# Feature sums of the key exponentials: from a DVE reduction to accumulating matmuls with the identity, under a new issue order

## The chip, the cores and the metric

The kernel runs on one core of one Trainium2 chip, as one launch. The metric is the device time of one execution in microseconds. Names of engines: PE is TensorE (PEld is its weight load), DVE is VectorE, ACT is ScalarE, POOL is GpSimd, and SP is the sync engine, which here issues nearly all DMAs.

## The reference

One input `u` (1 x 2048 x 512, bf16) feeds two branches, which a per-position gate mixes:

```python
x = A_u
g = sigmoid((x * gate_w).sum(-1, keepdims=True))
a = A(x, A_re, A_im, B_re, B_im, C_re, C_im, log_dt, Dskip)
b = B(x, wqkv, w_phi, wo)
return g * a + (1 - g) * b

def A(u, ...):                       # D=512, N=128, L=2048
    dt = exp(log_dt)[:, None]
    logdA, dB = dt * (A_re + 1j * A_im), dt * (B_re + 1j * B_im)
    K = einsum("dn,dnl,dn->dl", C, exp(logdA[:, :, None] * l), dB).real
    y = irfft(rfft(u padded to 2L) * rfft(K padded to 2L))[:L]
    return y + u * Dskip

def B(x, ...):                       # 32 heads, Dh=16
    q, k, v = x @ wqkv, split into heads
    pq, pk = q @ w_phi, k @ w_phi                       # per head
    phi_q = concat([softmax(pq), softmax(-pq)])         # over the head's 16 features
    phi_k = concat([softmax(pk), softmax(-pk)])
    kv, z = sum over s of phi_k x v, and of phi_k
    o = (phi_q @ kv) / (phi_q . z + 1e-6)
    return o @ wo
```

The change concerns the softmax denominators of `phi_k`: for each position, head and sign, the sum of 16 exponentials.

## The kernel before, in words

**How the order is made.** Each piece of work is a node of a `Plan` (`P.add(engine, cost, function, dependencies, take=rings, drop=rings)`). The costs and due times serve a planner that has been run beforehand. Its answer stands in the source as three strings: `ORDER` (two base-64 digits a node, the order of issue), `SIDES` (whether ACT or DVE does each eviction of PSUM by `evict`, lines 556 and 558), and `RINGS` (which PSUM ring a node takes: `ps` with two buffers, `p0` with two, `bk` with three, `pf` with two). On the chip each engine works through its own queue strictly in the order that `ORDER` gives; SP's queue of DMA issues is one of them. So a new string moves everything, on all engines.

**The stages**, as the order of before runs them:

- *Setup* (`prepare`, and the first part of `keys_and_spectrum`). SP loads `u` in four pieces (`UD`), loads the parameters B, C, A transposed (`nB`, `nC`, `nA`, line 292), loads the small tables and `Wv`, loads the query and key weights transposed (`wTq`, `wTk`, line 297), and loads `u` transposed as four `xT` blocks. PE multiplies `UD` with a table (`psA`, line 577), the result is evicted to `XAu`, multiplied again (`psB`, line 225), evicted to `XU` and written to a DRAM buffer `XUd`. DVE makes the tables, the parameter products (`pt`, line 425) and the folded key weights `Wkp` (evicted at line 556).
- *Keys* (the loop `for s2 in range(8)`, two tiles of 128 positions each, `u` = 0, 1). `pk` projects a tile (line 695, four matmuls of N=512 into a `bk` bank). `ex` makes two exponentials, exp(pk) and exp(-pk), each 128x512, into `Ek` (128 x 2 tiles x 2 signs x 512). `rd` reduces each 16 features of a head to one number on DVE (line 707), into `Zk`, 128 x 2 x 2 x 32 in fp32. `ln` takes the logarithm of the pair's `Zk` and then exp(-log), i.e. the reciprocal, into the last row of `vr`. `pv` projects the values (`vp`, line 727), an eviction copies them to `vb`, `sc` multiplies `vb` by the reciprocals into `vr` (line 736), and `kn` accumulates `kvp` with 32 small matmuls a tile (line 744).
- *The convolution kernel*, interleaved with the keys and queries: exponentials `E` and cosines `cs` of `args` on ACT, products `R` (lines 998 and 1001) and `A` (line 991) on DVE, and many small matmuls `kps` (line 212), evicted to `KD`.
- *Queries and convolution* (`queries_and_convolution`): query exponentials `Eq`, their denominators (`zs`, line 894), the transforms of the convolution (`psA`, `psB`, `psz` with evictions `XA`, `XK`, `Zr`), DMA round trips through DRAM (`XUd` to `U`, `Zr` to `Zd` to `ZT`), the attention output `bps` (lines 955 and 958), and the gated mix written out (`out_dram`).

The lines that the change touches, and those that call them:

Of the kernel before, what the change touches and what calls it, by code (L numbers as in the profile page):

```python
# [91 lines left out]
class Plan:  # L92


    DIGITS = "0123456789abcdefghijklmnopqrstuvwxyzABCDEFGHIJKLMNOPQRSTUVWXYZ-_"
    ORDER = ("050K0L0O0e0k0b08060v0M0N0001020h0n070f0c0g03090d0a0l0i0o0w0P0T0Q0m0R0y0z0q0B0U0V0S0-0Z0_100W1112132D16172F2H0X0Y141504"
             "18191a1b1c2E2G2I2J2K2L1p0j2M1q1u1t1d1i1e1f2N2P2R1j1r1v1z1s1k0p1w1y1A1B1N2O1E1C2S2Q1D1R1O1F1G1H1S2T1M2U2V2W2X2Z2_2Y1L2-"
             "1K1V1Q1g1T3031321h1l1W1I1U1x1P1m1J1X1Y0A1Z1-0s0x3335373438393a1_203b3c3d3f3e3g21220r3h3i3j3k2327243l3m3n3p3o3q2825292b"
             "2x2d3r3R0t0E0F3s2a2f3t2c2g2h3S2e3u3v3x3y3w2i2j2o2k2p1n2l2q263z3B363C3A2s2m2r0C2t2n0u0H0G2u3D3G3E3F0D2v3P0I0J2y2z3Q453H"
             "3I462A3J3K3M3N3O1o3L3U2B2w3X413V3Y3-442C3T4b4c4e4f4q4r4d4g4i4h4m4t4j4n4u638R8S4k4o4l4x4p4B4s4v474y4C4F424w4I8T4G4J8U97"  # L100
             "3W433Z4z4D4M4Q4R8V4H4K4L4A4E4U8W4N4V4X984O4Y4P4S4T575a585b9c4W4Z595c8X8Y4_494-50515d4a8Z919253545e5f8-93558_945i905j95"
             "963_525g99569a9b9e5m5n9B5k9d5p5q5t5h9f5u5x5l9g5B5o9m9C5r9o9n5s5v9h5y5z5C5D9i9p9r9D5E9E5w5I5M9t9j9k9F5J9l5A5F9q5G9G5Q5T"
             "5N5R9u9s5H5K5O5S5U9H5V9I9v9w5X5_5Y5W9J5Z605L615P9N5-629x9O9y649z9A9K6566aRaS9P6768696b6a406c6d6e6f9T9L9M6g6V9QaW9R9W9U"
             "a29VaPaQaU9S9Xa36h6i6Wa5aTa66j6k486m9Y9ZaX6laVadae6n9-9_a0a4a7aob2b4aYaZap6o6pagaf6qaqa-aha_a8bh6r6X6Za9aaai6s6t6u6vbi"
             "bjbkb0b36w6-b56_706x6Bb1b9arab6ya1b66Casb7b8babl6z6Ybm716Abb72ac73746F6G6D6E6J75atcvcwbc6K6L6H76776Ibdbe6McBajakcxcCbf"
             "bgauavbnbCbobDcDbz6Nbp6O78awbA797abBbEal7ebt7b7c7damanbKbucy7i6P7f6Q7g7j7h7mczbqbV6Rbrbv6T6S6U7k7nbLbMbWaxaybs7o7lbw7y"
             "bxbNbOby7zcE7p7AbF7CcAcMcF7E7B7D7FbPbGbHbI7q7G7Hc4c5bYbZ7IbXb-7J7KcN7L7s7M7NdjcG7Odk7PcP7u7rcHd17tcQ7w7vd2c7bQ7xc8bR7Q"
             "cO8b7RbJ7T7UcV8cbSc67Vc9cI8d8f8hcJ8ecKcRcS8gcT8i8j8kcL7ScUducW8l7W8mcX7XcY8ndl8ob_c0efegcZc_7_dv7Y7Zc-bTbUcad080cbdmdn"
             "8pc1dx7-d3dydw818qelccc2cd8r828s8w8tc3dod4dzeh8u83dp84ce8xdF8v8ydqdr8AdAd5dB8zdsdQ858Ed6d78B8C86dI8FdJ8GdGemen8D878HdR"
             "d8dTdHdKdCdDdEewd9dUexeydSdVdtddeH89deeiej88eIeJ8ada8Idf8KeodL8M8JdM8L8NdNdOdW8OdXdY8P8QazdZekdbepdgeqeresdceuetevf1dh"  # L110
             "aAf4f5cfaCaDezf2f3eAcgfaaBaEaFeKaKeLf6eBeMf7ciaGfbf8f9d-fifocjdPcheCfjeDaLeNckd_e0e2aHaIeOeEePaMclcmfkdifcfdfefgfhfffl"
             "frfmaNfscnaJaOeFeGcofpfncqcrcse1e5fqeQfteReSeVe3cpeTe4eWctfueUeaeXe6ebfwe7e8ecedeefvfxe9cueYeZfyfze-fAe_f0fBfC")
    SIDES = ("0100000011110011000000011000000100000000101110000000100000101000010000010000000100000000010000010000000000000011000000"
             "00000101001")
    RINGS = ("1100101101100100010000000000000000000022222222222222222222222222222222000002222222222222222222222222222222200000000000"
             "0000000000000000000300000000000000000000000300000000000000000000000330030333303330033")

    def __init__(self, rings, psum):
        self.k, self.dyn, self.nodes = dict(rings, **psum), set(psum), []
# [140 lines left out]
def prepare(P, tc, nc, g, evict, psum):  # L260

    fc, act, persist = g.fc, g.act, g.persist
# [20 lines left out]
    P.dma(1.1, 3.0, lambda: g.load_ld(), rw=("", "ldc ldb"))  # L283
    P.add("W", 7.0, lambda: None, rw=("raw0", "raw"))
    for dj in range(4):
        P.dma(0.6, 3.0, lambda dj=dj: g.load_ud(dj), rw=("", f"ud{dj}"), move=2.6)


    def turn(ks):
# [3 lines left out]
    for ks in (("Bre", "Bim"), ("Cre", "Cim"), ("Are", "Aim")):  # L293
        P.dma(2.6, 2.0, lambda ks=ks: turn(ks), rw=("", "n" + ks[0][0]), move=0.8)
    P.dma(2.5, 5.5, lambda: g.load_w(), rw=("", "wsm wv"))
    P.dma(2.2, 1.8, lambda: nc.sync.dma_start(out=g.wTk[:], in_=g.wsrc[:, 512:1024], transpose=True), rw=("", "wTk"), move=2.5)
    P.dma(2.2, 1.8, lambda: nc.sync.dma_start(out=g.wTq[:], in_=g.wsrc[:, 0:512], transpose=True), rw=("", "wTq"), move=2.5)  # L297
    xt = []

    for b in range(4):  # L300
        def xload(b=b):
            g.xT[b] = g.x4.tile([128, 4, 512], BF16, name="xT", tag="x4")
            for dj in range(4):
                nc.sync.dma_start(out=g.xT[b][:, dj, :].rearrange("p (t q) -> p t q", q=32),
                                  in_=g.UD[32 * dj:32 * dj + 32, 16 * b:16 * b + 16, :].rearrange("p t d -> p (t d)"), transpose=True)
        xt.append(P.dma(5.0, 2.0, xload, rw=("ud0 ud1 ud2 ud3", ""), take=["x4"], move=1.5))

    COS, SIN, MSIN = 6144.0, 4096.0, 0.0

# [93 lines left out]
    for qi, (k, mul) in enumerate((("Are", 1.0), ("Aim", 1.0 / TWO_PI))):  # L403
        v, h = 2 * qi, 2 * qi + 1
# [30 lines left out]
    x, y, are, aim, lg, r, ab, neg, u = (lambda i: (lambda: F.T[i][:]))(7), (lambda: F.T[8][:]), (lambda: F.T[2][:]), (lambda: F.T[4][:]), \  # L435
# [84 lines left out]
    kp = []  # L520
    for h in range(2):
# [14 lines left out]
        a = P.add("PE", 0.61, fb, [at_n], take=[("ps", "p0")], rw=("wTk", ""))  # L536
# [4 lines left out]
def keys_and_spectrum(P, tc, nc, g, psum):  # L541

    fc, act, at = g.fc, g.act, g.at
# [17 lines left out]
    polar, xt, kp, at_n = prepare(P, tc, nc, g, evict, psum)  # L561
    lnexp = P.add("ACT", 1.3, lambda: act.begin(LN_EXP), [polar], sets="L")

    gw, last, u0 = 32, [], []
    for h in range(2):
        X = Bag()
        en = []
        for g4 in range(gw // 4):
# [15 lines left out]
            a = P.add("PE", 1.0, pa, [a] if g4 else last, take=[("ps", "p0") if h == 0 else "ps"] + (["XAu"] if g4 == 0 else []), rw=("ud0 ud1 ud2 ud3 W1", ""))  # L584
            en.append(evict(ea, [a]))
        for r0 in range(0, 32, 4):
# [11 lines left out]
            a = P.add("PE", 0.75, pb, en + [a], take=[("ps", "p0") if h == 0 else "ps"], rw=("TB0 TB1 TB2", ""), drop=(["XAu"] if r0 == 28 else []))  # L598
# [12 lines left out]
    for h in range(2):  # L611
# [14 lines left out]
        a = P.add("PE", 0.61, fb, [at_n], take=[("ps", "p0")], rw=("wTq", ""))  # L626
# [19 lines left out]
    sp = P.add("X", 0.0, shift_psum, [n for n in P.nodes if n.psum is not None and not isinstance(n.psum.take[0], str)] + [polar], take=["acc"], opens="bk")  # L646
# [17 lines left out]
    a = P.add("PE", 1.8, ga, xt + [at_n], take=["ps"])  # L664
# [19 lines left out]
    for s2 in range(8):  # L684
        K = Bag()
        red = []
        for u in range(2):
            box = Bag()
            st = 2 * s2 + u
            ss = slice(128 * (st % 4), 128 * (st % 4) + 128)  # L690

            def pk(ss=ss, st=st, box=box):
                box.ps = bank("pk")
                for kt in range(4):
                    nc.tensor.matmul(box.ps[:], lhsT=g.xT[st // 4][:, kt, ss], rhs=g.Wkp[:, kt, :], start=(kt == 0), stop=(kt == 3))  # L695

            def ex(u=u, K=K, box=box):
                if u == 0:
                    K.E = g.kwk.tile([128, 2, 2, 512], BF16, name="Ek", tag="Ek")
                for sg in range(2):  # L700
                    act(out=K.E[:, u, sg, :], in_=box.ps[:], func=ACT.Exp, scale=(1.0 if sg == 0 else -1.0))
                box.ps = None

            def rd(u=u, K=K):
                if u == 0:
                    K.Z = g.kwk.tile([128, 2, 2, 32], F32, name="Zk")
                nc.vector.tensor_reduce(out=K.Z[:, u, :, :], in_=K.E[:, u, :, :].rearrange("p g (h f) -> p g h f", f=16),  # L707
                                        axis=mybir.AxisListType.X, op=ALU.add)
            a = P.add("PE", 1.05, pk, [a] if u else [sp, lnexp] + xt + kp, take=["bk"] + ([] if u else ["Ek", "Zk", "vr"]))
            x = P.add("ACT", 1.22, ex, [a] + ([x] if u else []), drop=["psum"], tab="L")  # L710
            red.append(P.add("DVE", 1.21, rd, [x] + red))

        def ln(K=K):
            K.v = g.kwk.tile([128, 2, 2, 17, 32], BF16, name="vr")
            act(out=K.Z[:], in_=K.Z[:], func=ACT.Ln)
            act(out=K.v[:, :, :, 16, :], in_=K.Z[:], func=ACT.Exp, scale=-1.0)
            K.Z = None
        l = P.add("ACT", 0.6, ln, red, drop=["Zk"], tab="L")
        for u in range(2):
            box = Bag()  # L720
            st = 2 * s2 + u
# [515 lines left out]
def full_kernel(tc, A_u, A_A_re, A_A_im, A_B_re, A_B_im, A_C_re, A_C_im, A_log_dt, A_Dskip,  # L1237
                B_x, B_wqkv, B_w_phi, B_wo, gate_w, out):
    nc = tc.nc
# [5 lines left out]
    with ExitStack() as ctx:  # L1245
# [110 lines left out]
        def shift_queries():  # L1356
# [70 lines left out]
```

## Time and profile before

| what | value |
|---|---|
| device time, 3 runs | 309.42, 314.25, 313.07 us (median 313.07) |
| the profiled execution | 311.04 us, of which the span from first to last instruction is 309.2 us |
| mean granted TensorE clock in it | 0.856 |
| busy, share of the span | DVE 249.2 us (81%), ACT 235.2 us (76%), PE 224.6 us (73%), PEld 137.9 us (45%), POOL 5.6 us (2%) |
| `Zk<-Ek`, the reductions of line 707 | 16 of 1213 ns mean, 18.9 us |
| `Ek<-pk`, the key exponentials | 32 of 610 ns mean, 16.9 us |
| `kvp<-vr,Ek`, line 744 | 512 matmuls of 199 ns mean |
| DMA | 39.88 MB, mean 129 GB/s |

How to read the profile: it records one execution. A busy share is an average over stages with different limits, so the stages are looked at by windows of time. A group of instructions is given as output<-input, with partitions x elements a partition and type; a matmul's duration is that of its passage through a pipeline, so consecutive matmuls overlap and their durations must not be added up. After a bar stands the idle time of the engine just before these instructions, and what ended most of it.

### The profile page before, as it was taken

The page shows a single profiled execution, that of the slowest core. Times are in us where ns is not written, and L with a number is a line of the kernel's source. Part 1 is how long each engine was busy: PE and PEld are TensorE (multiplying, and loading weights), DVE is VectorE, ACT ScalarE, POOL GpSimd, SP SyncE. Part 2 cuts the span into 40 slices and gives each one's busy share as a digit, 9 for nine tenths or more (in the row PEclk, how much of TensorE's full clock was granted, in tenths as well). Part 3 has the DMA queues.
Part 4 walks back from the last instruction along what each step waited for, and adds up shares of the span by engine and source line. Part 5 has one row for each costly group of instructions (what it writes and reads, how often), then busy time and mean ns, then how long its engine had stood idle before and what let it go on. Part 6 is the DMA issues. An engine that isn't in the chain of part 4 may idle for free.

```text
span 309.2 us, 10441 instructions
## 1 busy us (share of the span) xinstructions
PE 224.6 (73%) x4644; PEld 137.9 (45%) x4672; DVE 249.2 (81%) x400; ACT 235.2 (76%) x314; POOL 5.6 (2%) x17
## 2 busy tenths in 40 slices
PE   0052556655999689985987668999978996886980
PEld 0051545545345255552463543455644554444670
DVE  7709979999599979987987987798998696796641
ACT  3945997899799989997998859987987875643010
POOL 5000000000000000010000000000000000000000
PEclk9998577665799989996899989999999999577585
DMA  9995897867970000013024225613727657898364
GB/s 135 170 160 98 138 83 123 210 216 259 344 267 2 1 4 4 2 15 129 0 80 134 74 78 175 188 60 104 232 87 229 182 170 162 148 220 201 76 127 71
DMA packets 71357, 39.88 MB, mean 129 GB/s; under 512 B 57104, under 2 KB 63376, under 8 KB 71312
## 3 DMA queue, kind: packets, MB, share of 16 engines
q1 hardware_dynamic: 70256, 38.96, 52.5%
q8 instruction: 36, 0.59, 0.8%
q10 hardware_dynamic: 1056, 0.26, 0.6%
q14 instruction: 9, 0.07, 0.1%
HBM read 24.53 MB, written 14.94 MB: 128 GB/s over the span
## 4 chain that ended last, share of the span: by engine, by line
PE 30%; ACT 27%; DVE 21%; DMA 7%; SPq 7%; issue 6%; another core or an unknown queue 1%; DVEq 0%; ACTq 0%
PE bps L955 9%; PE kps L212 4%; ACT E L83 4%; ACT cs L83 3%; DVE A L991 3%; ACT Eq L83 3%; DMA pz<-pt 2%; ACT Zr L558 2%; DMA XUd<-XUd 2%; PE psB L1082 2%; PE psz L1118 2%; SPq L297 2%; DVE R L1001 2%; PE psz L1150 2%; SPq L292 2%
## 5 line engine op out<-in xcount | busy, mean ns | idle before, releaser
L991 DVE TENSOR_TENSOR A<-Ctab,Dtab 128x2048 bf16<-128x2048 bf16 x32 | 38.6, 1219 | 2.4 <-PE kps L212 2.4
L212 PE MATMUL kps<-R,A 128*32 128x64 bf16 x1536 | 26.6, 226 | 8.2 <-issue 2.6
L83 ACT ACTIVATE cs<-args 128x1024 bf16<-128x1024 f32 x32 | 30.8, 1043 | 1.4 <-PE args L791 1.3
L83 ACT ACTIVATE E<-args 128x1024 bf16<-128x1024 f32 x32 | 31.3, 1050 | 0.7 <-PE args L773 0.7
L577 PE MATMUL psA<-W,UD 128*64 128x256 bf16 x128 | 14.0, 369 | 23.9 <-DMA UD<-in_A_u_dram 18.5
L212 PEld LDWEIGHTS <-A 128*32 128x32 bf16 x1536 | 24.9, 153 | 11.4 <-issue 6.9
L955 PE MATMUL bps<-Mw,Eq 128*128 128x512 bf16 x122 | 29.4, 380 | 0.7 <-issue 0.6
L225 PE MATMUL psB<-XAu,TB 64*128 64x128 bf16 x256 | 14.1, 291 | 16.2 <-DVE XAu L556 7.5
L998 DVE TENSOR_TENSOR R<-E,cs 128x1024 bf16<-128x1024 bf16 x32 | 21.9, 686 | 4.6 <-PE kps L212 3.9
L577 PEld LDWEIGHTS <-UD 128*64 128x64 bf16 x128 | 11.4, 203 | 26.1 <-issue 25.9
L1001 DVE TENSOR_TENSOR R<-E,cs 128x1024 bf16<-128x1024 bf16 x32 | 22.0, 689 | 0.6
L707 DVE TENSOR_REDUCE Zk<-Ek 128x64 f32<-128x1024 bf16 x16 | 18.9, 1213 | 3.4 <-ACT Ek L83 3.4
L1104 DVE TENSOR_TENSOR t<-U,XK 128x1024 bf16<-128x1024 bf16 x28 | 17.8, 684 | 3.7 <-ACT XK L558 3.5
L225 PEld LDWEIGHTS <-TB 64*128 64x128 bf16 x256 | 12.4, 132 | 17.8 <-issue 9.5
L83 ACT ACTIVATE Ek<-pk 128x512 bf16<-128x512 f32 x32 | 16.9, 610 | 3.0 <-PE pk L695 3.0
L558 ACT CAST Zr<-psz 128x1024 bf16<-128x1024 f32 x13 | 13.3, 1021 | 7.5 <-PE psz L1118 6.2
L955 PEld LDWEIGHTS <-Eq 128*128 128x128 bf16 x128 | 11.5, 98 | 15.6 <-issue 3.4
L695 PE MATMUL pk<-Wkp,xT 128*128 128x512 bf16 x58 | 16.1, 408 | 2.8 <-DVE Wkp L556 2.0
L558 ACT CAST XA<-psA 128x1024 bf16<-128x1024 f32 x14 | 14.1, 1024 | 4.2 <-PE psA L1041 4.0
L83 ACT ACTIVATE Eq<-pq 128x512 bf16<-128x512 f32 x32 | 16.8, 638 | 0.0
L1118 PE MATMUL psz<-t,TI 128*128 128x512 bf16 x50 | 15.4, 412 | 1.9 <-ACT XK L558 0.7
L75 ACT ACT_TABLE_LOAD x12 | 15.4, 1283 | 0.9 <-PEq L1411 0.7
(180 smaller groups left out, 471.2 us busy)
## 6 DMA issues: line engine op xcount, KB each, us to landing
U<-XUd SPq DMA_DIRECT2D x16, 512.0 KB
XUd<-XUd SPq DMA_DIRECT2D x8, 512.0 KB
aexp<-apd SPq DMA_DIRECT2D x16, 256.0 KB
Zd<-Zr SPq DMA_DIRECT2D x14, 256.0 KB
XUd<-XU SPq DMA_DIRECT2D x8, 384.0 KB
ZT<-Zd SPq DMA_DIRECT2D x6, 512.0 KB
UD<-in_A_u_dram SPq DMA_DIRECT2D x4, 512.0 KB
out_dram<-o SPq DMA_DIRECT2D x32, 64.0 KB
```

Source lines behind the costliest of these rows:

```text
L83: i = self.nc.scalar.activation(**kw)
L212: nc.tensor.matmul(kps[32 * dj:32 * dj + 32, g4, e, :], lhsT=A[q][:, o, :, :, d].rearrange("p a b -> p (a b)"), rhs=R[ri][:, d, :], start= ...
L225: nc.tensor.matmul(ps[:, e, sl, :], lhsT=fc.TB[rows, r, 1 - ri:3 - ri, :].rearrange("p a b -> p (a b)"), rhs=XA[rows, r, ri, :], start=(ri ...
L558: nc.scalar.copy(out=o, in_=i)
L577: nc.tensor.matmul(box.ps[64 * e:64 * e + 64, i, :], lhsT=g.UD[:].rearrange("p t (e g) -> p g e t", e=2)[:, gw * h + 4 * g4 + i, e, :], rh ...
L707: nc.vector.tensor_reduce(out=K.Z[:, u, :, :], in_=K.E[:, u, :, :].rearrange("p g (h f) -> p g h f", f=16), axis=mybir.AxisListType.X, op= ...
L955: nc.tensor.matmul(box.ps[:], lhsT=Q.e[:, m, sg, 128 * i:128 * i + 128], rhs=g.Mw[:, 4 * sg + m, :], start=(k == 0), stop=False, skip_grou ...
L991: nc.vector.tensor_tensor(out=c.A[q][:].rearrange("p o a b d -> p (o a) b d"), in0=Ct.to_broadcast([128, 8, 8, 32]), in1=Dt.to_broadcast([ ...
L998: nc.vector.tensor_tensor(out=c.R[o][:, :, 32:64], in0=E[:, :, 32:64], in1=x, op=ALU.mult)
L1001: nc.vector.tensor_tensor(out=c.R[o][:, :, 0:32], in0=E[:, :, 0:32], in1=x[:, :, ::-1], op=ALU.mult)
L1104: nc.vector.tensor_tensor(out=o[:, k], in0=box.U[:, k], in1=box.XK[:].rearrange("p s (o d) -> p o s d", o=no), op=ALU.mult)
L1118: nc.tensor.matmul(box.ps[:, hb], lhsT=fc.TI[:, k].rearrange("p t h a -> p (t h a)"), rhs=rhs, start=(k == 0), stop=(k == 1))
```

## The change

The node `rd` is removed and with it the `Zk` tile and ring. In its place a node `ks` on PE follows the pair's second exponential: 16 matmuls, all with the 128 x 128 identity as the stationary operand, the f-th with the columns f, f+16, f+32, ... of the pair's `Ek` as the moving one (128 columns), accumulating into one PSUM tile `kz` of 128 x 128 in fp32, taken from ring `bk` or `ps`. `ln` takes its logarithm in place in PSUM and reads it there for the reciprocal. Line numbers behind that place are larger by one than before.

Four groups of planner costs are changed as well, and the three strings are new throughout (cut here). With them, each engine's order differs from the first instructions on: SP issues the four `UD` loads (with two small ones between) first, then other small loads and `Wv`, then the transposed loads of C, B and A, and then `wTq`, `wTk` and the `xT` blocks, where before nC came ahead of the second half of `UD`, and `wTq` ahead of nB. Six evictions of 128x1024 and seven of `vb` that ACT did are now done by DVE. In two places PE has the 16 matmuls of two pairs in a row.

```diff
-    ORDER = ("050K0L0O0e0k0b08060v0M0N0001020h0n070f0c0g03090d0a0l0i0o0w0P0T0Q0m0R0y0z0q0B0U0V0S0-0Z0_100W1112132D16172F2H0X0Y141504"
...
+    ORDER = ("0K0N0L080b02000M050601040e0q0k0h0n0O0P030-0Z0Q0R0S0_0T100f0U110V0W070g090a120c1316170Y1415180d190X1a1b2D2F0r0v2H0o1c2x"
...
-    SIDES = ("0100000011110011000000011000000100000000101110000000100000101000010000010000000100000000010000010000000000000011000000"
...
+    SIDES = ("0010000000110111000011000011010000101111111000101011000010001000010001010001001100000000000001100010000001100000010000"
...
-        P.dma(0.6, 3.0, lambda dj=dj: g.load_ud(dj), rw=("", f"ud{dj}"), move=2.6)
+        P.dma(0.7, 2.0, lambda dj=dj: g.load_ud(dj), rw=("", f"ud{dj}"), move=2.75)
...
-    P.dma(2.2, 1.8, lambda: nc.sync.dma_start(out=g.wTk[:], in_=g.wsrc[:, 512:1024], transpose=True), rw=("", "wTk"), move=2.5)
+    P.dma(4.7, 1.8, lambda: nc.sync.dma_start(out=g.wTk[:], in_=g.wsrc[:, 512:1024], transpose=True), rw=("", "wTk"), move=2.5)
...
-            def rd(u=u, K=K):
-                if u == 0:
-                    K.Z = g.kwk.tile([128, 2, 2, 32], F32, name="Zk")
-                nc.vector.tensor_reduce(out=K.Z[:, u, :, :], in_=K.E[:, u, :, :].rearrange("p g (h f) -> p g h f", f=16),
-                                        axis=mybir.AxisListType.X, op=ALU.add)
-            a = P.add("PE", 1.05, pk, [a] if u else [sp, lnexp] + xt + kp, take=["bk"] + ([] if u else ["Ek", "Zk", "vr"]))
+            a = P.add("PE", 1.05, pk, [a] if u else [sp, lnexp] + xt + kp, take=["bk"] + ([] if u else ["Ek", "vr"]))
             x = P.add("ACT", 1.22, ex, [a] + ([x] if u else []), drop=["psum"], tab="L")
-            red.append(P.add("DVE", 1.21, rd, [x] + red))
+            red.append(x)
+
+        def ks(K=K):
+            K.Z = (bank("kz") if P.cur.ring == "bk" else psum([128, 512], "kz"))[:, 0:128]
+            for f in range(16):
+                nc.tensor.matmul(K.Z, lhsT=g.ident[:], rhs=K.E[:].rearrange("p u s (h f) -> p f (u s h)", f=16)[:, f], start=(f == 0), stop=(f == 15))
 
         def ln(K=K):
             K.v = g.kwk.tile([128, 2, 2, 17, 32], BF16, name="vr")
-            act(out=K.Z[:], in_=K.Z[:], func=ACT.Ln)
-            act(out=K.v[:, :, :, 16, :], in_=K.Z[:], func=ACT.Exp, scale=-1.0)
+            act(out=K.Z, in_=K.Z, func=ACT.Ln)
+            act(out=K.v[:, :, :, 16, :], in_=K.Z.rearrange("p (u s h) -> p u s h", u=2, s=2), func=ACT.Exp, scale=-1.0)
             K.Z = None
-        l = P.add("ACT", 0.6, ln, red, drop=["Zk"], tab="L")
+        q = P.add("PE", 1.05, ks, red, take=[("bk", "ps")])
+        l = P.add("ACT", 0.6, ln, [q], drop=["psum"], tab="L")
```

More of the change, by code (lines that the diff above doesn't have):

```diff
@@ L95 @@
     DIGITS = "0123456789abcdefghijklmnopqrstuvwxyzABCDEFGHIJKLMNOPQRSTUVWXYZ-_"
-    ORDER = ("050K0L0O0e0k0b08060v0M0N0001020h0n070f0c0g03090d0a0l0i0o0w0P0T0Q0m0R0y0z0q0B0U0V0S0-0Z0_100W1112132D16172F2H0X0Y141504"
[L97 to L112, printed above, removed]
@@ L113 @@
-    SIDES = ("0100000011110011000000011000000100000000101110000000100000101000010000010000000100000000010000010000000000000011000000"
-             "00000101001")
-    RINGS = ("1100101101100100010000000000000000000022222222222222222222222222222222000002222222222222222222222222222222200000000000"
-             "0000000000000000000300000000000000000000000300000000000000000000000330030333303330033")
+    ORDER = ("0K0N0L080b02000M050601040e0q0k0h0n0O0P030-0Z0Q0R0S0_0T100f0U110V0W070g090a120c1316170Y1415180d190X1a1b2D2F0r0v2H0o1c2x"
+             "2E2G1d1i1j1p0l0i1e0j0m1t1u0p1k2I1f1q2J2K1r1v1s1w1x2L2M2N2P2O2Q2R2S2T2V2X1z1y1Q1A1S2W1O2Z1B1L1P2_1R2U2Y1N1C1E30311D2-1F"
+             "0s1G1H321K0t331T341M351g3738393a3b0u1V1l0w1U1W1I1m3c3d3f1X3e1h1Y3g1J1Z1-3h1_3i203j3l3k0x3m2122233n3o3p3q3r3s3t27282924"
+             "362a3u2b253v2c3w3x3y2A2f2g2h2i2d2B2j3R2e2k3z3A3B3C3S0y2l2o2p2n0B2q0E0F3D1n3G0H0I0J3H260C3E0D3J3M3K3I2m0z0G0A451o2s2r2u"
+             "2t2y463P3L2z3F3N2v2w3Q3O41423X442C4b3-3_3Y3T5X47484c4d4e4p4q4f4h434g404i4j8J8K4l4m4n8L8M4r8_8N8O4k904o4D3U4E494F4s4a94"
+             "3V3W8P4G8Q4t4u4H4I4v8R8V4w4z4x4A4J4B4K4L8W8S8X4N4O914P92968T4y4C4R8Y8U8Z8-4T3Z4X9t4M934S4Y4U4Q534V544W9u954_979e4Z9g50"
+             "515556989v99594-9w5a5d9h57585b529f5e9a5f9b9j9l5h5c5i5j9c9d9x5n5o5g5k5l5r5s9i5v5m5p5q5t5x5u9m9kaH9y5w5y9z9A5J5B5K5C5L9n"
+             "5M9o5zaI5F5N5A5D5P5G9B5H5Q5O5R5T5E5I5S9F9C9G5U5V9H5W5Y9D9I5ZaJaKaO5-9p9q5_60616362646566679L9W9M9E9J9K9r9s68699N6a6b9O"
+             "b99Pba6c6daL6eaM6f9Qa5a69Z9-aN6N6g6h6OaP9XaYaQ6Pa79Y6i6jaR6k6lbbbc9R9S6RaSaTa8a96TaU6S6UaV6Q6m6n6o9_ag6p6t6u6qaZaWaXa-"
+             "b19Ta_bdbe6rb09U6V6vb26s9V6x6W6X6Y6w6Zcn6yb3b4b5aacoa06-b66Bbf6_a1bgabacajah6z6A6Cctbh6Da270717273a3brbsaiak6E6Fblbmcp"
+             "b774cua4alcv767778cq6G6Hbib8bj6IbnbobC757acr797e7b7ccwbD6Jbk6Lbu7qbpbqbv6M6KbFbGcs7samadcx7rae7uan7dbE7f7g7h7tao7vafcy"
+             "7w7x7iczbtbw7j7ybQ7zbxapaqcEcFbNbObPbRbHcG7A7BbS7k7C7DbYdbbI7E7FbybJ7l7mcHcI7ncKcL7GcA7obzbAbKbLb_bZbBb-7H7L7McBdccNcM"
+             "7p8385877I7J7Nc0c18486dm7K7P897QcC88cJ8a8bcOcPcD8c8d8e7ObT8f7TcQcRbUcScT8g8hbMc2cUdec3dddndodf7RbVbW7S8i8jdpcV7Ue77V7W"
+             "dge87XdqcW7YbX8k8o8l8mc4c58p8qe9dA8ndr8rdh8sc6edee7Z8tdB8w8xefdi7-cXcYdxcZdI7_dj8u8yc_c-d081dsdL8v8zdkdydJ8AdKdMdtdldz"
+             "dCeodudN80ezeAepeB8Beqd18C828Ed58Gd68Fea8D8H8Iarc7ebd2audvavdwasd7egc8awd3c9atdDecehdOdEeVdPd8caeWcbccdQeiejekelemdFeX"
+             "dGend4axdRdSd9e_f0eYereCayeZf2eseteDe-f3daeEaCdHazf1cdaDeuevf4f5f6f8fafgdTewceaEcfcgeFf9f7exeycheGdUfhaAaBciaFdVfdfjaG"
+             "dZeHfbfccjfkdWfefffifld-eIfmfoeJeKdXdYeNckcld_fne0eLcmeMeOe2ePfpe1e3eQe4fqeRe5eSeTeUfrfsftfue6")
@@ L118, in __init__ @@
+    SIDES = ("0010000000110111000011000011010000101111111000101011000010001000010001010001001100000000000001100010000001100000010000"
+             "00000010110")
+    RINGS = ("1001011101011011010000000000000000010022222220222222222222220222222222222222220000022222222222222222222222222222222000"
+             "000000000000000000000000000000000000000000000000000030000000000030000000303000033303330330333")
     def __init__(self, rings, psum):
@@ L295, in prepare @@
     P.dma(2.5, 5.5, lambda: g.load_w(), rw=("", "wsm wv"))
-    P.dma(2.2, 1.8, lambda: nc.sync.dma_start(out=g.wTk[:], in_=g.wsrc[:, 512:1024], transpose=True), rw=("", "wTk"), move=2.5)
-    P.dma(2.2, 1.8, lambda: nc.sync.dma_start(out=g.wTq[:], in_=g.wsrc[:, 0:512], transpose=True), rw=("", "wTq"), move=2.5)
+    P.dma(4.7, 1.8, lambda: nc.sync.dma_start(out=g.wTk[:], in_=g.wsrc[:, 512:1024], transpose=True), rw=("", "wTk"), move=2.5)
+    P.dma(4.7, 1.8, lambda: nc.sync.dma_start(out=g.wTq[:], in_=g.wsrc[:, 0:512], transpose=True), rw=("", "wTq"), move=2.5)
     xt = []
@@ L305, in xload @@
                                   in_=g.UD[32 * dj:32 * dj + 32, 16 * b:16 * b + 16, :].rearrange("p t d -> p (t d)"), transpose=True)
-        xt.append(P.dma(5.0, 2.0, xload, rw=("ud0 ud1 ud2 ud3", ""), take=["x4"], move=1.5))
+        xt.append(P.dma(5.3, 2.0, xload, rw=("ud0 ud1 ud2 ud3", ""), take=["x4"], move=1.5))
     COS, SIN, MSIN = 6144.0, 4096.0, 0.0
@@ L1361, in full_kernel @@
         g.shift_keys, g.shift_queries = shift_keys, shift_queries
-        P = Plan({"XAu": 1, "Ek": 2, "Zk": 2, "vr": 2, "vb": 2, "acc": 1, "r8": 2, "nrm": 1, "ax": 2, "x4": 5, "o": 3, "E": 4, "cs": 4, "A": 3, "R": 3, "KD": 1, "XA": 2,
+        P = Plan({"XAu": 1, "Ek": 2, "vr": 2, "vb": 2, "acc": 1, "r8": 2, "nrm": 1, "ax": 2, "x4": 5, "o": 3, "E": 4, "cs": 4, "A": 3, "R": 3, "KD": 1, "XA": 2,
                   "XK": 2, "Z": 2, "Zr": 2, "U": 2, "t": 2}, {"ps": 2, "p0": 2, "bk": 3, "pf": 2})
```

## The prediction

> **What bounds the kernel now.** I read the busy shares first, then the chain that ended last, then the busy time by stage.
>
> ```profile
> PE 224.6 (73%) x4644; PEld 137.9 (45%) x4672; DVE 249.2 (81%) x400; ACT 235.2 (76%) x314; POOL 5.6 (2%) x17
> PE 30%; ACT 27%; DVE 21%; DMA 7%; SPq 7%; issue 6%; another core or an unknown queue 1%; DVEq 0%; ACTq 0%
> ```
>
> DVE is the busiest, but the chain spends only 21% on it: three engines hand the end to one another, so 1 us off DVE is worth 1 us only where DVE ends a wait. Windows cut at the first key projection, the end of the keys, the first query exponential and the tail give (columns: length, then busy us of PE, PEld, DVE, ACT, POOL, clock, DMA share, GB/s):
>
> ```profile
> 0.00:77.30 77.30, 33.34 (x480) 28.85 (x480) 62.09 (x139) 60.56 (x69) 4.69 (x16) 0.76 0.87 159
> 77.30:138.30 61.00, 53.92 (x1240) 28.27 (x1252) 53.61 (x68) 56.69 (x94) 0.84 (x1) 0.95 0.23 80
> 138.30:154.40 16.10, 11.65 (x132) 5.40 (x137) 13.65 (x29) 14.29 (x15) 0.11 (x1) 0.79 0.23 67
> 154.40:277.00 122.60, 106.08 (x2047) 60.82 (x2054) 103.51 (x150) 98.26 (x134) 0.00 (x0) 0.93 0.51 144
> ```
>
> In the setup DVE sets the end (it works almost without a gap once its transposed loads are there). In the key stage, where the change is, **ACT** is fullest (56.7 of 61.0), with PE at 53.9 and DVE at 53.6 close behind. So the reduction removed is no bottleneck of its stage, while matmuls added to PE fall on an engine with 7 us to spare, if ACT waits for them.
>
> ```profile
> L707 DVE TENSOR_REDUCE Zk<-Ek 128x64 f32<-128x1024 bf16 x16 | 18.9, 1213 | 3.4 <-ACT Ek L83 3.4
> L83 ACT ACTIVATE Zk<-Zk x8: 293/313/414, 83.2 to 135.8; 128x128 f32<-128x128 f32 x8
>   ACT Zk L83: 0.8, 2
> ```
>
> Sixteen reductions of 1.21 us. Of those who waited for them (last line, us and times) ACT's logarithm waited 0.8 us in all: today it is nearly free.
>
> [...](1213 ns for 1024 elements a partition, where the tensor_tensor L998 takes 686). [...](four diagD matmuls, N=128, in 0.32 us, 80 ns each). [...]in the sources' min/median/max ns:
>
> ```profile
> L212 PEld LDWEIGHTS <-A x1536: 131/153/168, 109.3 to 279.8; 128*32 128x32 bf16 x192
> L744 PEld LDWEIGHTS <-Ek x512: 92/102/120, 85.2 to 138.0; 128*32 128x32 bf16 x171
> L744 PE MATMUL kvp<-vr,Ek x512: 189/199/212, 85.3 to 138.1; 128*32 128x34 bf16 x171
> L577 PEld LDWEIGHTS <-UD x128: 184/205/218, 18.4 to 53.9; 128*64 128x64 bf16 x128
> L958 PE MATMUL bps<-diagD,xT x64: 219/219/219, 190.6 to 256.6; 128*128 128x128 bf16 x64
> ```
>
> 32 adjacent columns load in 92 ns; 32 columns strided by 64 bytes (A) in 131, 64 strided by 256 bytes (UD) in 184: (184−131)/32 = **1.66 ns per strided column**. Moving operands lie on 165 + 0.416 N ns (N=1 gives 165, 128 gives 219, 512 gives 379); kvp, N=34 in 17 separate pairs, should take 179 and takes at least 189, its tenth percentile 193: 14/17 = 0.8 ns on top of the 0.83 of a pair[...]. So a kz matmul holds PE for 128 × 1.67 = **213 ns** and shows 165 + 213 ≈ 379 ns; 16 make **3.4 us a group**, eight groups 27 us. Bounds: were a step of 32 bytes free, 56 to 80 ns each, 0.9 to 1.28 us a group (8 to 10 us in all); half the penalty, 107 ns, 1.7 us. I take 213, because two other operands give the same slope; the other values stay as cases.
>
> **The change part by part.**
>
> Removed: 16 reductions at a pitch of 1.13 us, 18.1 us of DVE. But the new assignment of evictions gives DVE six more of 128x1024 (XU +3, XA +3, Zr +1, XAu −1; 1.14 us each) and seven vb (0.6): +11.0, net −7.1. ACT loses them: 6 × 0.90 + 7 × 0.50 = −8.9. PE gains 128 matmuls. The loads of the identity (some 98 ns like L958's) lie beside the matmuls and are free at 213 ns[...]. Logarithm and exponential now work on PSUM: same 128x128 size, 0.31 us each as in the row shown; from −0.1 to +0.1 each, taken as nothing.
>
> Setup, to the first pk (77.3). Its waits:
>
> ```profile
> 22.57 0.69 DVE L425 TENSOR_TENSOR pt<-nCre,nBre 128x512 f32<-128x512 bf16 x1 [7.49 <-DMA nBre<-in_A_B_re_dram]
> 18.46 2.83 PE L577 MATMUL psA<-W,UD 128*64 128x256 bf16 x24 [18.46 <-DMA UD<-in_A_u_dram]
> ```
>
> SP's issue order is turned: the four UD loads first, then the small loads, Wv, and only then the nC, nB, nA transposes; wTq and wTk after these, then xT. Each transposing issue holds SP (nC 4.67 us, wTq 6.21 before). [...]the trace has nB at 22.57, after UD at 18.46. So UD comes slightly earlier (about 17) and nB later: I take 24.7, with 21 to 27. DVE then has less behind nB: of its 51.1 us after 22.57, the attention constants 2.2, two parameter steps 2.0 and one XAu 1.1 are done while waiting, and 2.3 of extra evictions come: 51.1 − 5.3 + 2.3 − 0.7 (rest of small moves) = 47.4, and some 3 us idle (3.6 now) give 24.7 + 47.4 + 3 = 75.1. The first pk needs Wkp, just ahead of that end: 74.5, **−2.8** (−7 if nB comes early and UD's start is used, +1 if nB is at 27 and the wait shows elsewhere).
>
> Keys to the first query exponential (77.3 to 154.5 = 77.2 us). ACT's work here was 70 us; less seven vb (3.5) and two XA (1.8): 64.7. DVE's falls from 67.8 to 55, so DVE ends nothing here. PE takes its queue in order: the 16 kz matmuls stand behind the pk of the group and ahead of vp, of the next args and kps. ACT too is in order: its Ln stands behind the Exp of the group (often the next group's two as well) and ahead of the next E or cs exponentials, so ACT stands still until the 16 are done. Walking along ACT's new order, with each kz group starting when its last Ek and PE's earlier entries are done and less what ACT still has ahead of Ln, gives seven waits (two groups stand as 32 matmuls in a row): 2.7, 2.7, 1.8, 2.4, 3.7, 2.5, 2.9 = 18.7 us. With 1.1 for pk to Ek and 5.3 for the last Mw evictions before Eq: 64.7 + 1.1 + 5.3 + 18.7 = 89.8, **+12.6**. At 80 ns the same walk gives waits of 4.3, so 75.4, −1.8; at 107 ns 6.8, 77.9, +0.7. The bypassed wait of 0.8 us for the reduction is within this.
>
> From Eq to the end (154.5 on): the same progress is made at its start. DVE has 3.4 us more (XA, Zr, one A product), ACT 1.8 less, the A and R products (L991, L998, L1001) lead DVE there: **+1** (−4 to +6, as an order written anew can lose or gain a wait per block; the XUd, U, Zd and out issues on SP are spread with slack). Changed planner costs act only through the order.
>
> Sum against the profiled execution (311.04 us, span 309.2, so 1.8 around it): −2.8 + 12.6 + 1 = +10.8, **321.8 us**. The median of the runs, 313.07, is 2 us above that execution; I don't add it.
>
> **Rivals.**
> 1. *The stride is free* (80 ns): −2.8 − 1.8 + 1 = −3.6, 307.4; and should the early UD shorten the setup by its 7 instead of 2.8 and no more be lost later, 303 to 305: faster, on the other side. It decides from a kz group of about 1.3 us down. For it: 32 bytes is less than the 64 and 256 measured. Against it: both slopes are alike[...].
> 2. *Half the penalty* (107 ns): −2.8 + 0.7 + 1 = −1.1, 310: no change.
> 3. *The price is right and the setup is late too*: nB at 27 or a later xT brings +4 where I have −2.8: 328.6.
>
> That the sums aren't done by PE is no rival: the instructions are in the changed program, 8 × 16, each with 128 columns at a step of 16 elements.
>
> **How the numbers follow.** My forecast 0.55 (322, own range 314 to 330), rival 3 0.17, rival 2 0.10, rival 1 0.18. A measurement of this kernel tells about 2%, 6.3 us on 313.07. Faster by that (under 306.8) needs rival 1 with the early setup: 0.12. Slower (over 319.3): about 0.55, from the forecast's upper two thirds (0.39) and rival 3 (0.16). Same: 0.33. The range 307 to 332 takes in most of rival 1, all of rival 2, and rival 3.
>
> **What would show it.** kz matmul: 379 ns mean against 219; a group 3.4 us against 1.3. ACT's row kz<-kz waiting for PE kz: some 19 us in seven to eight waits, against 4. nB's wait on DVE ending near 24.7; first pk at 74.5; first Eq near 164 against 150 to 153. DVE with clear idle time between those two. I am wrong if kz shows 220 ns, or if it shows 379 and ACT does not wait because its queue has work ahead of Ln that I placed wrongly; and the last stage is wrong if Eq to the end differs from before's by more than 6 us.

## The result, and the profile after

The changed kernel takes 337.93 us (median of four runs, 334.82 to 339.05) against 311.25 us (median of four): ratio 1.093, 95% interval 1.079 to 1.107. The ratios in this text leave out executions more than 1.5% above the fastest of their kernel, here those of before with 313.07 and 314.25 us; the two medians as they stand give 1.086. The sign was forecast, the size was not: 322 us, with a range that ended at 332. The profiled execution took 334.82 us (span 333.0), 23.8 us more than that of before; forecast were 10.8.

Busy times, and the chain of waits by engine, from the page of the changed kernel:

```profile
PE 256.6 (77%) x4768; PEld 151.9 (46%) x4800; DVE 242.9 (73%) x397; ACT 227.7 (68%) x301; POOL 5.0 (1%) x17
PE 49%; DVE 22%; ACT 14%; DMA 6%; issue 5%; SPq 4%; DVEq 0%; ACTq 0%
```

DVE and ACT lost about the work that was counted (6.3 and 7.5 us, forecast 7.1 and 8.9), PE gained 32 us, and its share of the chain went from 30% to 49%. The stages, cut at the same events as before (first pk, end of the keys, first Eq, tail; columns: length, busy us of PE, PEld, DVE, ACT, POOL, clock, DMA share, GB/s):

```profile
0.00:71.58 71.58, 32.80 (x480) 28.37 (x481) 62.75 (x140) 58.33 (x67) 4.00 (x16) 0.76 0.91 168
71.58:161.70 90.12, 85.74 (x1230) 42.07 (x1242) 43.78 (x62) 52.85 (x84) 0.00 (x0) 0.82 0.18 57
161.70:180.31 18.61, 15.33 (x207) 6.08 (x207) 12.43 (x27) 15.02 (x17) 0.95 (x1) 0.69 0.18 58
180.31:303.00 122.69, 105.35 (x2158) 61.93 (x2169) 111.90 (x157) 97.28 (x132) 0.00 (x0) 0.96 0.51 144
```

The setup is 5.7 us shorter (71.6 against 77.3), what follows the first Eq 2.0 us shorter (152.7 against 154.7). All the loss lies between the first pk and the first Eq: 108.73 us against 77.16, so +31.6. There PE is now the fullest engine (85.7 of 90.1), and the mean clock of the key part, 0.95 before, is 0.82.

Groups of the changed kernel (busy us, mean ns, and behind the bar the idle time ahead of them with what ended it):

```profile
L711 PE MATMUL kz<-Ek,ident 128*128 128x128 bf16 x128 | 30.8, 411 | 0.8 <-ACT Ek L83 0.8
L83 ACT ACTIVATE kz<-kz 128x128 f32<-128x128 f32 x8 | 2.1, 263 | 19.2 <-PE kz L711 15.3 <-issue 3.9
L728 PE MATMUL vp<-Wv,xT 128*128 128x512 bf16 x60 | 21.6, 492 | 0.5 <-issue 0.4
L556 DVE CAST vb<-vp 128x512 bf16<-128x512 f32 x11 | 7.6, 690 | 23.1 <-PE vp L728 23.1
```

A kz matmul shows 411 ns (forecast 379), a group of 16 lasts 3.87 us; start to start it is 231 ns. ACT's waits ahead of its logarithm of kz are 19.2 us (for 3.9 of them the profile names no releaser), where the prediction's walk along ACT's order gave 18.7. The third row is what the prediction did not have: the value projections, untouched, went from 380 to 492 ns on average. In the kernel before they were:

```profile
L727 PE MATMUL vp<-Wv,xT 128*128 128x512 bf16 x59 | 15.3, 380 | 0.4 <-issue 0.2
```

The timeline of PE in the changed kernel shows where they grow longer:

```profile
79.70 1.04 PE L728 MATMUL vp<-Wv,xT 128*128 128x512 bf16 x4
...
88.93 7.58 PE L711 MATMUL kz<-Ek,ident 128*128 128x128 bf16 x32 [0.52 <-ACT Ek L83]
96.34 1.89 PE L728 MATMUL vp<-Wv,xT 128*128 128x512 bf16 x4
```

The same four matmuls take 1.04 us behind the first group of kz and 1.89 us behind the double one. Windows laid at the changes of the granted clock (it is the third column from the end) say why:

```profile
88.93:91.41 2.48, 2.48 (x11) 1.27 (x11) 0.00 (x0) 2.48 (x4) 0.00 (x0) 1.00 0.00 0
91.41:101.65 10.24, 10.24 (x35) 4.10 (x33) 1.99 (x3) 4.58 (x8) 0.00 (x0) 0.50 0.00 0
101.65:111.00 9.35, 9.24 (x257) 4.71 (x261) 8.05 (x14) 8.13 (x10) 0.00 (x0) 1.00 0.02 4
```

PE is busy all the time from 88.93 to 101.65, and yet the clock is halved from 91.41 on: 2.5 us into 32 strided matmuls. The kz matmuls themselves don't slow down (231 ns on both sides of the change), what stands behind them does. From the first Ek to the first Eq the clock is at half for 42 of 106.8 us by the trace's record of it, in the kernel before for 11.5 of 75.2.

### The profile page after: what moved, and what is told of

It is laid out like the page before. It is cut to its first block, busy times and chain, and to the rows that moved or that the text cites. A ratio compares the mean times of both kernels' runs of the same rounds, so it can differ in the third digit from the quotient of the medians.

```text
span 333.0 us, 10673 instructions
## 1 busy us (share of the span) xinstructions
PE 256.6 (77%) x4768; PEld 151.9 (46%) x4800; DVE 242.9 (73%) x397; ACT 227.7 (68%) x301; POOL 5.0 (1%) x17
## 4 chain that ended last, share of the span: by engine, by line
PE 49%; DVE 22%; ACT 14%; DMA 6%; issue 5%; SPq 4%; DVEq 0%; ACTq 0%
PE kz L711 8%; PE kps L212 6%; PE bps L956 6%; PE vp L728 5%; DVE A L992 3%; PE pk L695 3%; ACT E L83 3%; PE args L792 2%; PE psz L1119 2%; DMA wc<-in_B_w_phi_dram 2%; PE pq L880 2%; PE psA L1042 2%; DVE R L1002 2%; PE psB L1083 2%; SPq L1298 2%
## 5 line engine op out<-in xcount | busy, mean ns | idle before, releaser
L711 PE MATMUL kz<-Ek,ident 128*128 128x128 bf16 x128 | 30.8, 411 | 0.8 <-ACT Ek L83 0.8
L212 PEld LDWEIGHTS <-A 128*32 128x32 bf16 x1536 | 24.7, 152 | 11.1 <-issue 8.9
L737 DVE TENSOR_TENSOR vr<-vb,vr 128x1024 bf16<-128x1024 bf16 x16 | 11.0, 692 | 19.6 <-ACT vr L83 18.0
L556 DVE CAST vb<-vp 128x512 bf16<-128x512 f32 x11 | 7.6, 690 | 23.1 <-PE vp L728 23.1
L711 PEld LDWEIGHTS <-ident 128*128 128x128 bf16 x128 | 15.1, 120 | 15.4 <-issue 2.1
L728 PE MATMUL vp<-Wv,xT 128*128 128x512 bf16 x60 | 21.6, 492 | 0.5 <-issue 0.4
L225 PE MATMUL psB<-XAu,TB 64*128 64x128 bf16 x256 | 13.3, 276 | 10.1 <-DVE XU L556 4.7
L558 ACT CAST Zr<-psz 128x1024 bf16<-128x1024 f32 x12 | 12.2, 1016 | 12.4 <-issue 6.1
L695 PE MATMUL pk<-Wkp,xT 128*128 128x512 bf16 x56 | 17.6, 433 | 3.2 <-ACT Wkp L558 2.1
L956 PEld LDWEIGHTS <-Eq 128*128 128x128 bf16 x128 | 11.8, 98 | 15.3 <-issue 3.0
L225 PEld LDWEIGHTS <-TB 64*128 64x128 bf16 x256 | 11.5, 124 | 11.9 <-issue 11.8
```

Of the source, the lines that this page charges most:

```text
L212: nc.tensor.matmul(kps[32 * dj:32 * dj + 32, g4, e, :], lhsT=A[q][:, o, :, :, d].rearrange("p a b -> p (a b)"), rhs=R[ri][:, d, :], start= ...
L225: nc.tensor.matmul(ps[:, e, sl, :], lhsT=fc.TB[rows, r, 1 - ri:3 - ri, :].rearrange("p a b -> p (a b)"), rhs=XA[rows, r, ri, :], start=(ri ...
L711: nc.tensor.matmul(K.Z, lhsT=g.ident[:], rhs=K.E[:].rearrange("p u s (h f) -> p f (u s h)", f=16)[:, f], start=(f == 0), stop=(f == 15))
L956: nc.tensor.matmul(box.ps[:], lhsT=Q.e[:, m, sg, 128 * i:128 * i + 128], rhs=g.Mw[:, 4 * sg + m, :], start=(k == 0), stop=False, skip_grou ...
```

## Experiments

All take the changed kernel as their base, unless said otherwise; the column "order" says whose issue order runs. Times are medians. Ratios are to the kernel before, timed again beside each batch (its medians were 311.5 to 311.9 us), with 95% intervals; two kernels were run once only.

| kernel | kz on PE, per group | order | us | ratio |
|---|---|---|---|---|
| changed | 16, step 16 | new | 337.9 | 1.093 (1.079 to 1.107) |
| e1 | 16, adjacent | new | 306.1 | 0.981 (0.974 to 0.988) |
| e2 | none, DVE reductions | new | 309.8 | 0.994 (0.990 to 0.999) |
| e3 | 16 of N=512, adjacent | new | 325.7 | 1.042 (1.034 to 1.051) |
| e4 | eight patterns | new | 311.9 | one run |
| e5 | 4 of N=512, then DVE | new | 309.4 | 0.993 (0.991 to 0.996) |
| e6 | 32, step 4 | new | 326.3 | one run |
| e7 | 16, step 16 | before's | 348.6 | 1.114 (1.108 to 1.120) |
| e8 | 16, step 16, split | new | 333.9 | 1.072 (1.068 to 1.077) |
| e9 | 4 of N=512, then DVE | before's | 325.0 | 1.039 (1.033 to 1.045) |
| e10 | 16, step 16, and 4 dense | new | 344.0 | 1.106 (1.098 to 1.113) |

**e1: the step alone.**

```diff
-rhs=K.E[:].rearrange("p u s (h f) -> p f (u s h)", f=16)[:, f]
+rhs=K.E[:].rearrange("p u s x -> p (u s x)")[:, 128 * f:128 * f + 128]
```

> The changed kernel in its own order, with one edit: each of the 16 kz matmuls reads 128 adjacent columns of Ek instead of every 16th, so it adds up other elements; number, size and place of all instructions stay. Theory (the step of the moving operand starves PE, and the clock that is granted falls behind each group): a kz matmul at 219 ns, a group at about 1.3 us instead of 3.87, ACT's waits for kz under 5 us instead of 19, hardly any time at half clock in the key stage outside what before had, first Eq near 152, total near 306 us. Rival (the new order as such costs it): kz short, but the key stage still longer than before, total 325 or more.

Measured: 306.1 us; kz 222 ns, 56 ns start to start, first Eq at 150.2 (in its profiled execution, the longest of its four with 309.5 us; where its surplus of 3 us lies isn't known). ACT hardly waits any more:

```profile
L83 ACT ACTIVATE kz<-kz 128x128 f32<-128x128 f32 x8 | 2.3, 289 | 0.7 <-PE kz L711 0.6
```

So the step of the moving operand, with what it brings about, is worth 32 us (337.9 against 306.1); nothing else was changed but which elements are added up.

**e2: the new order without kz.** `ks` left empty, the `tensor_reduce` of before behind each pair of exponentials.

> The changed kernel's order, with the 16 kz matmuls of a group taken out and the two reductions on DVE back, each right behind its pair of exponentials. Theory (kz is the whole cost): the key stage back near 77 us, the setup's gain of 5.7 us kept, total 303 to 309 us. Rival (order): total 320 or more. If DVE, which has 13 evictions more in this order, now ends the waits in the key stage, 310 to 316.

Measured: 309.8 us, between the first range and the third. The setup's gain is there (first Ek at 73.7 against 79.2), but from there to the first Eq it takes 80.7 us where before took 75.2: the gain is given back. DVE's busy time in the windows from first pk to first Eq is 73.3 us (67.3 before), and ACT's logarithm waits 3.9 us for the reductions instead of 0.8. The order is no part of the loss. The clock is at half for 21.0 us of those 80.7, without a kz matmul; its mean is 0.87 up to 136.0 and 0.81 from there to the first Eq, and PE has gaps there (busy 67.4 of 82.6 us from the first pk on).

**e4: the price of a step.** One pattern in each group:

```diff
+            st = (1, 2, 4, 8, 16, 0, 0, 0)[s2]
...
+                nc.tensor.matmul(z, lhsT=g.ident[:], rhs=r, start=(f == 0), stop=(f == 15))
```

> The changed kernel with another moving pattern in each of the eight groups, 128 columns always: step 1, 2, 4, 8, 16 elements; then 64 pairs, 32 quads, and 4 runs of 32 adjacent elements (the sums are of other elements in all but the fifth). Theory [...]: start to start 56 to 80 ns for steps 1, 2 and 4, about 230 for 8 and 16, about 116 for pairs, 80 or less for quads and runs. Rival (a price for any step over one element): 230 for steps 2 and 4 too. Rival (growing with the step): 8 clearly below 16.

Start to start, 128 columns each, from the start times in the trace:

| pattern | ns |
|---|---|
| adjacent | 56 |
| step 2 | 60 |
| step 4 | 116 |
| step 8 | 227 |
| step 16 | 232 |
| 64 pairs, 64 bytes apart | 110 |
| 32 quads | 56 |
| 4 runs of 32 | 56 |

Quads and runs of 32 take as long as adjacent columns (56 ns), step 2 little more (60), step 4 and the pairs about twice as long (116 and 110), steps 8 and 16 about four times (227 and 232). So there is no one price for any step over one element, and from step 8 on the time hardly grows further: at step 16 it is 1.81 ns a column. Why the patterns differ, no view shows. Of the eight patterns step 4 missed the forecast, with 116 ns against 56 to 80; the others came out as it said. All eight are from one execution.

**e3 and e6: the same hold of PE with the array in use for longer.** The hold is the time for which a group keeps PE. PE's array is called in use here for the time that adjacent columns took (56 ns for 128 of them, e1), and starved when the matmuls follow one another more slowly than that; no view shows the array itself. In both kernels the sums are of other elements. e3 reads 512 adjacent columns in each of the 16 matmuls. e6 has 32 matmuls at step 4:

```diff
-            for f in range(16):
-                nc.tensor.matmul(..., rhs=K.E[:].rearrange("p u s (h f) -> p f (u s h)", f=16)[:, f], ...)
+            for f in range(32):
+                o = 512 * (f // 8) + f % 4
+                nc.tensor.matmul(..., rhs=K.E[:].rearrange("p u s x -> p (u s x)")[:, o:o + 509:4], ...)
```

> The changed kernel, but each kz matmul reads 512 adjacent columns (the sums are of other elements): at full clock 213 to 216 ns each, so a group holds PE for about 3.6 us, nearly as long as the strided group (3.87), but with PE's array working all the time. Theory [...]: no half-clock windows behind the groups, pk and vp at 379 ns, total near 318 us, what my walk gave for that length of group. Rival A (only the length of the groups counts, the clock falls for another reason): total within 3 us of the changed kernel's 335 to 338. Rival B (the identity as stationary operand, mostly zeros, lowers the clock): half-clock windows stay, and then a group is longer than 6 us.

> The changed kernel with 32 matmuls a group instead of 16, each with 128 columns at a step of 4 elements (the sums are of other elements): 116 ns each as measured with that step, so a group holds PE for 3.7 us as the changed kernel's does, but the array is in use 46% of that time instead of 23%. If the clock falls with the share of time in which the array is in use, and the limit lies below 46%: no half-clock windows, total 323 to 327 us. If any starved stream lowers the clock: 335 us, windows as in the changed kernel.

Measured: 325.7 and 326.3 us. For e3 that is 8 us above what was expected (318), though the clock did as expected there. In e6 a group holds PE for 32 x 116 = 3.7 us, as in the changed kernel (16 x 231); in e3 it is 3.6. The windows of their key parts, e3 first:

```profile
71.98:152.00 80.02, 77.60 (x1231) 37.84 (x1243) 43.71 (x62) 52.34 (x84) 0.00 (x0) 0.98 0.20 63
72.20:153.00 80.80, 79.51 (x1359) 54.72 (x1370) 43.53 (x62) 52.47 (x85) 0.00 (x0) 0.98 0.19 62
```

And the groups of e6:

```profile
L729 PE MATMUL vp<-Wv,xT 128*128 128x512 bf16 x59 | 15.6, 381 | 0.4 <-issue 0.2
L83 ACT ACTIVATE kz<-kz 128x128 f32<-128x128 f32 x8 | 2.1, 263 | 18.2 <-PE kz L712 14.9 <-issue 2.7 <-ACT E L83 0.6
```

Clock 0.98 against 0.82, vp at 381 ns against 492, ACT's waits for kz nearly as in the changed kernel (18.2 against 19.2). First Eq comes at 168.4 instead of 180.3. So of the stage's excess over e1 (31.0 us from first Ek to first Eq: 106.8 against 75.9) 18.6 us belong to the hold of PE (94.4 in e6) and 12.4 us to the fallen clock; e3, with 93.7 us, gives 13.1 for the clock. Over whole kernels the medians say nearly the same, 11.6 us (e6) and 12.2 (e3). The profiled executions differ by 8.5 us only, as e6's took 3.5 us longer from Eq on. The identity as stationary operand is not the cause of the fall: e3 and e6 have it too.

**e8 and e10: two attempts to keep the clock up.** e8 cuts each group into 5, 6 and 5 and draws the next entries of PE's queue between (`if f in (4, 10): P.pull()`). e10 puts a matmul of N=384 over adjacent columns behind every fourth strided one.

> The changed kernel with each kz group cut into pieces of 5, 6 and 5 matmuls, and the next one or two entries of PE's queue (value projections, args, kps) drawn forward between the pieces where their inputs are there; the work is the same, all matmuls strided. Theory [...]: the matmuls drawn in keep the array in use, fewer half-clock windows in the key stage, total 322 to 331 us though each sum is ready later. Rival (the clock falls for the total of strided matmuls, or the length of the groups is all): 335 us or more.

> The changed kernel with one matmul more behind every fourth strided one: 384 adjacent columns of Ek into the unused part of the same PSUM bank, never read. A group then holds PE for about 4.4 us instead of 3.7, and the array is in use for some 34% of it instead of 23%. If 34% is enough to keep the clock: no half-clock windows behind the groups, and in spite of 32 matmuls more, total 328 to 333 us, faster than the changed kernel. If it isn't: 339 to 345 us. The length of the group alone, at 0.8 us of stage for each us of hold, adds about 4 us.

e8: 333.9 us (332.7 to 336.1), 4 us below the changed kernel (334.8 to 339.1), and between the two ranges that were expected. The clock of its key part is 0.90, against 0.82 in the changed kernel. But each sum is ready later, and ACT now waits longer for it, which takes back most:

```profile
L83 ACT ACTIVATE kz<-kz 128x128 f32<-128x128 f32 x8 | 2.1, 262 | 29.4 <-PE kz L723 23.8 <-issue 5.6
```

e10: 344.0 us, as forecast for the case that a third isn't enough. The clock of its key part is 0.86, above the changed kernel's 0.82 but far from the 0.98 of e6, and ACT waits 19.3 us for PE's kz where it waited 15.3.

**e7: strided kz in before's order.** The 16 matmuls stand where the pair's second reduction stood.

> The kernel before in its own order, with only the reductions replaced: the 16 strided kz matmuls of a group stand on PE where the pair's second reduction stood on DVE. Theory (kz with its step is the cost, not the new order): 330 to 340 us, kz matmuls of 412 ns, half-clock windows behind the groups. Rival (the order has a good part in the loss): under 325 us.

Measured: 348.6 us, above the range. The strided sums in place of the reductions cost 37 us in the old order (311.9 beside it) and 28 in the new one (309.8 in e2): the new order absorbs part of what they cost. From first Ek to first Eq it is 111.7 us against 75.2.

**e5 and e9: a reading in runs of four.** Four adjacent features at a time, in the layout that is there:

```diff
+            for i in range(4):
+                nc.tensor.matmul(box[:].rearrange("p (j r) -> p j r", r=4), lhsT=g.ident[:],
+                                 rhs=K.E[:].rearrange("p u s (h f) -> p (u s h) f", f=16)[:, :, 4 * i:4 * i + 4], start=(i == 0), stop=(i == 3))
+            nc.vector.tensor_reduce(out=..., in_=box[:].rearrange("p (j r) -> p j r", r=4), axis=mybir.AxisListType.X, op=ALU.add)
```

> The changed kernel with the same sums from another reading of Ek: four accumulating matmuls of N=512 a group, the i-th with the four adjacent features 4i to 4i+3 of each head[...]; the four partial sums a head are then added by one DVE reduction, 128x128 from 128x512 in PSUM. Theory (what costs is the moving operand's step, and four adjacent elements are free): 216 ns a matmul, a group 1.0 us on PE and 0.65 us on DVE, no half-clock windows behind the groups, 304 to 308 us, faster than before by 1 to 2%. Rival (the additional step from PE to DVE to ACT costs as much as it saves): 309 to 313 us.

> The kernel before in its own order, with the two reductions of a pair replaced by the four N=512 matmuls over four adjacent features and one DVE reduction of 128x128 from 128x512 in PSUM. DVE saves 16 x 1.21 - 8 x 0.69 = 13.9 us of busy time, PE gets 8 groups of about 1.0 us. If DVE's reductions cost the kernel before nothing (ACT waited 0.8 us for them): 309 to 313 us. If DVE's time in the key stage counts: 300 to 306 us.

e5: 309.4 us, 0.7% faster than before (interval clear of 1), level with e2; of all kernels here only e1, which adds up other elements, was faster. That is in the range of the rival, not of the theory. The hold is 1.08 us a group instead of 3.87. A matmul follows after 230 ns, not 216 as with the 512 adjacent columns of e3. What the additional hand-over adds in waits:

```profile
L711 PE MATMUL kz<-Ek,ident 128*128 128x512 bf16 x32 | 8.6, 392 | 0.9 <-ACT Ek L83 0.8
L714 DVE TENSOR_REDUCE Zk<-kz 128x128 f32<-128x512 f32 x8 | 5.5, 691 | 11.5 <-PE kz L711 11.5
L83 ACT ACTIVATE Zk<-Zk 128x128 f32<-128x128 f32 x8 | 2.6, 327 | 4.3 <-DVE Zk L714 4.2
```

e9, the same in before's order, missed both expectations: 325.0 us. DVE's reductions wait 25.9 us for PE there, ACT 7.4 us for them:

```profile
L712 DVE TENSOR_REDUCE Zk<-kz 128x128 f32<-128x512 f32 x8 | 5.5, 691 | 25.9 <-PE kz L709 25.9
L83 ACT ACTIVATE Zk<-Zk 128x128 f32<-128x128 f32 x8 | 2.5, 308 | 7.4 <-DVE Zk L712 7.4
```

The first kz matmul of a group starts 1.4 us after the group's last Ek on average, in e5 1.6; so PE comes to the sums no later than there. But this order, written for Ek to DVE, brings DVE to the reduction earlier, and its whole queue stands behind the wait. That this makes up the 13 us was not tried by itself. One microsecond of PE work a group cost 13 us in an order that had no place for it, and nothing in the order that had (e5 against e2).

## Why the prediction was right or wrong

By its own steps, profiled execution against profiled execution:

- **Price of the strided operand: right in kind, 8% low.** Forecast 213 ns start to start and 379 ns shown; measured 231 and 411. The slope of 1.66 ns a strided column, taken from weight loads and kvp, is 1.81 for this operand (232 ns for 128 columns, e4). Eight groups hold PE 2.3 us longer than forecast.
- **ACT waits for kz: right, in part by luck.** Forecast 18.7 us, measured 19.2, in seven waits as forecast. But with the measured hold the walk's own rate would give 20.6; single waits came out otherwise (the second 1.2 where it had 2.7, the third 3.1 where it had 1.8). e1 and e6 confirm the rate: 8 x (3.7 − 0.9) = 22.4 us more hold of PE lengthen the stage by 18.6, 0.83 us each; the walk had (18.7 − 4.3) / (27.3 − 10.2) = 0.84.
- **The step that failed: the walk along ACT's order, "each kz group starting when its last Ek and PE's earlier entries are done", has no term for a change in how long these other entries (vp, args, kps, pk) take.** They grow longer at the lower clock (four vp matmuls 1.89 us at 0.50, 1.04 at 1.00), and the clock was taken as given. It fell behind the strided groups, and vp took 492 ns instead of 380; that is worth 12.4 us (e6 against the changed kernel) and alone lifts 321.8 beyond the range. Rival 3 (328.6) came nearest, for a wrong reason: the setup was not late but early.
- **The walk's base was short.** First pk to first Eq at nearly full clock with the same hold is 96.3 us in e6, forecast were 89.8 for a hold 0.3 us a group shorter, which at 0.83 us is 1.9; 4.6 us are left. Of these 2.6 are ACT's own work: between these two points ACT is busy for 67.3 us in e6 (67.9 in the changed kernel), where the prediction had 64.7. One of the 2.6 is in its sum: its windows show ACT busy for 56.7 + 14.3 = 71.0 us before, and it starts from 70. (It also takes DVE's 67.3 as 67.8, on which nothing rests.) The other 2.0 are waits; e6 has ACT wait 6.1 us for vp and 1.5 for args, which the walk did not have. Which of them count was not tried.
- **The setup: right sign, too small.** −2.8 forecast, −5.7 measured, and the mechanism was wrong in part. The trace has DVE at the first product with nB at 23.52, without a wait; I had the load itself arrive at 24.7 and DVE idle until then. DVE's one long wait is 3.6 us for wc at 18.5, and in the whole setup it is idle for 8.8 us instead of 15.2. Nor did UD come at about 17: PE's first product with it starts at 18.32, before 18.46.
- **From Eq on:** +1 forecast, −2.0 measured, inside the −4 to +6. The other kernels with the new order take 152.3 to 157.5 us there, so not even the sign is shown.
- **The rivals on the other side** (free stride, half the penalty) fall: e4 has 232 ns, no cover. The 80 ns taken for a free stride was no pace either: the four diagD matmuls start 56 ns apart in the trace of before, as those of e1 do, and the 0.32 us run to the start of the next matmul.

So the miss of the total, 23.8 − 10.8 = 13.0 us, divides into 12.4 (clock) + 1.9 (price) + 4.6 (base) − 2.9 (setup) − 3.0 (from Eq on). The base is what the other terms leave over, so the sum is no proof of them.

How the clock falls is only partly settled. In the traces of before and of the changed kernel its record has 1.00 and 0.50 and nothing between, in stretches of 3.41 us or whole multiples of it, but for the last one, which ends with the record. A PE that is busy in the profile doesn't keep it up: it is busy without a gap from 88.93 to 101.65, and the clock is at 0.50 from 91.41 on. The share of time in which the array is in use fits better. Estimated from the measured paces, it is 56 of 231 ns (24%) in a strided group, about a third in e10, 56 of 116 ns (48%) in e6 and all of it in e3; the clock of the key part is 0.82, 0.86, 0.98 and 0.98 in this order. Nor does it take a strided matmul: e2 has none, PE with gaps, and a clock of 0.87. What the clock follows, and whether there is a limit between a third and 48%, these runs don't show.

## What to carry to other kernels

Before moving a sum to PE, look at how the elements of each moving operand lie: in these runs the step was free or nearly so with runs of 4 adjacent bf16 elements (56 ns for 128 columns, 230 instead of 216 for 512), and a step of 8 made the matmul four times as long (227 ns). Ask also what a slow stream does to its neighbours: here four dense matmuls behind the strided ones took 1.89 us at a clock of 0.50 instead of 1.04, although PE was not idle in between. And judge an operation and its order together: kz cost 37 us in one order and 28 in the other, the quads 13 us and nothing.

## What the runs showed of the hardware that was not expected

- A kz matmul at step 16 takes the same 231 ns at a clock of 1.00 and of 0.50 (the group at 88.93 ran through the change without altering its pace), while four dense vp matmuls behind it took 1.89 us instead of 1.04.
- A higher busy share of PE can go with a lower clock: 95% busy at 0.82 in the changed kernel's key part, 88% at 0.95 before.
- The logarithm and exponential on PSUM took 262 and 278 ns where those on SBUF took 313 and 309: 0.08 us less for each pair, 0.7 us in all.
